# Earlier release of a batch's loads, its last keys in two pieces, and its TensorE steps spread over two output units, in a fused attention and SwiGLU kernel

## The chip, the cores and the metric

One core of one Trainium2 chip runs the whole program. The metric is the device time of one execution in microseconds. The granted clock, the share of TensorE's full speed that the profile records, has a mean of 0.99 to 1.00.

## The reference

An attention without a softmax over pairs feeds a gated feed-forward block.

```python
q_s = exp(q - max_d);  q_s /= sum_d            # softmax of each query over its 64 features
k_s = exp(k - max_s);  k_s /= sum_s            # softmax of the keys over the 576 positions
kv  = einsum('bhsd,bhse->bhde', k_s, v)        # 64 x 64 for each head
x   = einsum('bhsd,bhde->bhse', q_s, kv)       # laid out as 4608 tokens x 512
out = (silu(x @ w_gate) * (x @ w_val)) @ w_out # 512 -> 1536 -> 512
```

There are 8 batches of 8 heads, 576 positions and 64 features. Inputs are float32; the kernel computes in bfloat16 on TensorE (PE).

## The kernel before

Work is written in the order in which each engine takes it. Batch 0's 576 tokens go first, through twelve units (called m-units): each has a gate and a value product into two PSUM banks, which ScalarE (ACT, the silu `sg`) and VectorE (DVE, the product `hr`) then empty. After that comes the stretch that the change rewrites: the four output projections of batch 0's first 512 tokens, with batch 1's attention between them. Then follows the first regular chunk (448 tokens), into which batch 2's attention is worked.

```python
psp = ctx.enter_context(tc.tile_pool(name="psp", bufs=8, space=PSUM))   # 8 banks, used in turn
...
def load_kv(b):
    for G in range(NG):                       # NG = 2 groups of four heads
        load("k", k, b, G)
        load("v", v, b, G)
...
for c0, n in ((0, 128), (128, 128), (256, 128), (384, 128), (512, 256), (768, 384), (1152, 384)):
    w_slice(wg, moe_w_gate, c0, n)            # GpSimd queue, float32 -> bf16 on the way
    w_slice(wv, moe_w_val, c0, n)
w_dma = [wo_slice(m0, 3) for m0 in (0, 3, 6, 9)]
...
after = w_dma[-3]                             # batch 1's loads wait for the 2nd output-weight slice
for what, src in (("q", q), ("v", v), ("k", k)):
    for G in range(NG):
        load(what, src, 1, G, after=after)
        after = None
load("q", q, 2, 0); load("q", q, 2, 1); load_kv(2)

for m in range(MT):
    m_unit(0, S, m, by_group=(m == 0))        # batch 0: twelve units

exp_of("q", 1, 0); exp_of("q", 1, 1)          # ACT, after a switch of its function table
norm_sum(1, 0); i = norm_mul(1, 0)            # DVE; norm_mul writes qs
cast_v(1, 0)
c = cast_v(1, 1)                              # GpSimd (POOL), float32 -> bf16
tc.add_manual_dep(c.ins, i.ins.name, ...)     # second cast after the first product
norm_sum(1, 1)
o_out(0, o_mm(0), nc.scalar); o_out(1, o_mm(1), nc.scalar)
exp_of("k", 1, 0)
turn_pe(1, 0, 0); turn_pe(1, 0, 1)            # PE transposes of qs
...
kv_both(1); scale_both(1)                     # keys x values, then kn on DVE
...
exp_of("k", 2, 0); exp_of("k", 2, 1)          # before ACT switches its table to silu
...
for m in range(MT):                           # the first chunk (ci == 0)
    ...                                       # m == 5: kv_both(2); m == 6: exp_of("k", 3, 0), ("k", 3, 1)
    m_unit(c0, n, m, by_group=(ci == 0 and m == 0))
    if att and m == 9:
        x_and_next_kv(b)                      # the x step, with the next batch's keys x values
```

In the profiles `eq` and `ek` are the exponentials of queries and keys, `qs` the normalised queries, `qt` their transposes, `vb` the values in bfloat16, `kv` and `kn` the key-value product before and after its scaling, `xp` the x step and `xt` its result; `g_ps`, `u_ps` and `o_ps` are PSUM banks of the gate, value and output products.

The softmax here doesn't subtract the row's maximum and nothing guards it: scores larger than these inputs give would overflow.

Of the kernel before, what the change touches and what calls it, by code (L numbers as in the profile page):

```python
# [15 lines left out]
def kernel(  # L16
# [10 lines left out]
    nc = tc.nc  # L27
# [5 lines left out]
    MT = d_ff // 128  # L33
    T = S // 64
# [3 lines left out]
    BANKS = ((0, 5), (5, T))  # L38
# [8 lines left out]
    def bank(name):  # L47
        return psp.tile([128, 512], FP32, tag="ps", name=name)
# [16 lines left out]
    def head_ap(src, b, G, t0=0, t1=T):  # L65
        return bass.AP(
            tensor=src.tensor,
            offset=src[b, 4 * G].offset + 64 * t0,
            ap=[[T * 64, 128], [2 * HSTR, 2], [1, (t1 - t0) * 64]],
        )  # L70

    def load(what, src, b, G, pieces=((0, T),), after=None):
        t_ = ld.tile([128, 2, T * 64], FP32, tag=what, name=what)
        raw[what, b, G] = t_
        last = None
        for t0, t1 in pieces:
            last = nc.sync.dma_start(out=t_[:, :, 64 * t0:64 * t1], in_=head_ap(src, b, G, t0, t1))  # L77
            if after is not None:
                tc.add_manual_dep(last.ins, after.ins.name, SYNC, reason="order of loads")
                after = None  # L80
        return last
# [6 lines left out]
    def w_slice(dst, src, c0, n):  # L88
        ap = bass.AP(
            tensor=src.tensor,  # L90
            offset=src[0, c0].offset,
            ap=[[d_ff, 128], [128 * d_ff, KT], [1, n]],
        )
        return nc.gpsimd.dma_start(out=dst[:, :, c0:c0 + n], in_=ap)  # L94

    def wo_slice(m0, n):
        ap = bass.AP(
            tensor=moe_w_out.tensor,
            offset=moe_w_out[m0 * 128, 0].offset,
            ap=[[d_model, 128], [128 * d_model, n], [1, d_model]],  # L100
        )
        return nc.gpsimd.dma_start(out=wo[:, m0:m0 + n, :], in_=ap)

    def copy(eng, out, in_):
        if eng is nc.scalar:
            nc.scalar.copy(out=out, in_=in_)
        else:
            eng.tensor_copy(out=out, in_=in_)  # L108
# [3 lines left out]
    st = {}  # L112

    def exp_of(what, b, G, pieces=((0, T),)):
        s = st.setdefault((b, G), {})
        e = s["e" + what] = at.tile([128, T, 2, 64], BF16, tag="e" + what, name="e" + what)
        src = raw[what, b, G].rearrange("p h (t d) -> p t h d", d=64)
        for t0, t1 in pieces:
            nc.scalar.activation(out=e[:, t0:t1], in_=src[:, t0:t1], func=AF.Exp)  # L119
# [34 lines left out]
    def turn_pe(b, G, i):  # L154
        s = st[b, G]
        if i == 0:
            s["qt"] = at.tile([128, T, 128], BF16, tag="qt", name="qt")
        t0, t1 = BANKS[i]
        tp = s["tp", i] = psp.tile([128, 1024], BF16, tag="ps", name="tp")
        for t in range(t0, t1):  # L160
            j = t - t0
            nc.tensor.transpose(
                out=tp[:, j * 128:(j + 1) * 128], in_=s["qs"][:, t, :], identity=ident
            )

    def turn_out(b, G, i, eng):
        s = st[b, G]
        t0, t1 = BANKS[i]
        copy(
            eng,  # L170
            s["qt"][:, t0:t1, :],
            s["tp", i][:, 0:(t1 - t0) * 128].rearrange("p (t c) -> p t c", c=128),
        )
# [8 lines left out]
    def kv_mm(b, G, kv, c):  # L182
        ek = st[b, G]["ek"]
        for t in range(T):
            for g in range(2):
                for h in range(2):
                    nc.tensor.matmul(  # L187
                        out=kv[g][HALF[h], c:c + 65], lhsT=ek[HALF[g], t, h, :],
                        rhs=vbs[G][HALF[g], t, h, :],
                        start=(t == 0), stop=(t == T - 1),  # L190
                    )
# [23 lines left out]


    def kv_both(b):
        kv = st["kv", b] = [bank("kv") for _ in range(2)]
        for G in range(NG):
            kv_mm(b, G, kv, 256 * G)  # L220

    def scale_both(b):
        kn = st["kn", b] = at.tile([128, 2, NG, 64], BF16, tag="kn2", name="kn2")
# [67 lines left out]
    def store(j, o_sb, c0=0, c1=512, engs=(nc.sync, nc.sync)):  # L291
        for half in range(2):
            b, t = divmod(2 * j + half, T)
            dst = bass.AP(
                tensor=out.tensor,
                offset=out[b * S + t, c0].offset,
                ap=[[T * d_model, 64], [1, c1 - c0]],
            )
            engs[half].dma_start(out=dst, in_=o_sb[64 * half:64 * half + 64, c0:c1])

    def o_mm(j, o_ps=None, m0=0, m1=MT):
        if o_ps is None:
            o_ps = bank("o_ps")
        r0 = (j * 128) % RING
        for m in range(m0, m1):
            nc.tensor.matmul(  # L306
                out=o_ps, lhsT=hr[:, m, r0:r0 + 128], rhs=wo[:, m, :],
                start=(m == 0), stop=(m == MT - 1),
            )
        return o_ps  # L310

    def o_out(j, o_ps, eng=nc.vector):
        o_sb = osb.tile([128, 512], FP32, tag="o_sb", name="o_sb")
        copy(eng, o_sb, o_ps)
        store(j, o_sb)

    def o_unit(j):
        o_out(j, o_mm(j))
# [17 lines left out]
    with tc.manual_schedule():  # L336
# [23 lines left out]
        norm_mul(0, 0, BANKS)  # L360
        norm_sum(0, 1, BANKS)

        for c0, n in ((0, 128), (128, 128), (256, 128), (384, 128), (512, 256), (768, 384), (1152, 384)):
            w_slice(wg, moe_w_gate, c0, n)
            w_slice(wv, moe_w_val, c0, n)
        w_dma = [wo_slice(m0, 3) for m0 in (0, 3, 6, 9)]
# [67 lines left out]
        x_out(0, 1, 0, xp1[0])  # L434
        x_out(0, 1, 1, xp1[1])

        after = w_dma[-3]
        for what, src in (("q", q), ("v", v), ("k", k)):
            for G in range(NG):
                load(what, src, 1, G, after=after)  # L440
                after = None
        load("q", q, 2, 0)
        load("q", q, 2, 1)
# [13 lines left out]
        o_out(0, o_mm(0), nc.scalar)  # L457
        o_out(1, o_mm(1), nc.scalar)
        exp_of("k", 1, 0)
        turn_pe(1, 0, 0)  # L460
        turn_pe(1, 0, 1)
        turn_out(1, 0, 0, nc.scalar)
        exp_of("k", 1, 1)
        norm_mul(1, 1)
        p = o_mm(2)
        turn_out(1, 0, 1, nc.vector)
        turn_pe(1, 1, 0)
        turn_pe(1, 1, 1)
        turn_out(1, 1, 0, nc.scalar)
        turn_out(1, 1, 1, nc.vector)  # L470
        kv_both(1)
        scale_both(1)
        o_out(2, p, nc.scalar)
        exp_of("q", 2, 0)
        p = o_mm(3, m1=MT // 2)
        x_and_next_kv(1, with_kv=False)
        o_mm(3, p, m0=MT // 2)
        o_out(3, p)
        exp_of("q", 2, 1)
        norm_sum(2, 0)  # L480
        norm_mul(2, 0)
# [9 lines left out]
        for ci, (c0, n) in enumerate(chunks):  # L491
            b = ci + 2
            jo = 4 * ci
            att = b < B
            more = b + 1 < B
            final = ci == len(chunks) - 1
            for m in range(MT):
                if ci == 0:
                    if m == 3:
                        norm_mul(b, 1)  # L500
                        turn_dma(b, 1)
                    elif m == 5:
                        kv_both(b)
                        scale_both(b)
                    elif m == 6:
                        exp_of("k", b + 1, 0)
                        exp_of("k", b + 1, 1)
                        cast_v(b + 1, 0)
                        cast_v(b + 1, 1)
                elif m == 3:  # L510
                    if att:
                        exp_of("q", b, 0)
                        exp_of("q", b, 1)
                        norm_sum(b, 0)
                    o_unit(jo)
                    if att:
                        norm_mul(b, 0)
                        turn_dma(b, 0)
                    o_unit(jo + 1)
                    if att:  # L520
                        norm_sum(b, 1)
                elif m == 4 and att:
                    norm_mul(b, 1)
                    turn_dma(b, 1)
                elif m == 7:
                    if more:
                        exp_of("k", b + 1, 0)
                        exp_of("k", b + 1, 1)
                        cast_v(b + 1, 0)
                        cast_v(b + 1, 1)  # L530
                    o_unit(jo + 2)
                    if not final:
                        o_unit(jo + 3)
                if m == 8 and more:
                    for G in range(NG):
                        load("q", q, b + 1, G)
                    if b + 2 < B:
                        load_kv(b + 2)
                m_unit(c0, n, m, by_group=(ci == 0 and m == 0))
                if att and m == 9:  # L540
                    x_and_next_kv(b)
        o_unit(jo + 3)
        last = n_tok // 128 - 4
# [33 lines left out]
```

## Time and profile before

| what | before | view |
|---|---|---|
| time, median of the first 3 runs | 313.84 us | runs |
| PE busy | 97% of the span | page |
| stretch of output units | 37.81 to 52.47 us, 14.66 us | PE timeline |
| its first m-unit to the next chunk | 52.47 to 73.08 us, 20.61 us | PE timeline |
| batch 2's last keys land | 54.9 us | issue plus latency of that load |

The page of the kernel before: busy time of the engines in us with its share of the span and the number of instructions (PEld is TensorE's loading of weights), then the chain of waits by engine.

```profile
PE 301.5 (97%) x2158; PEld 150.6 (48%) x2182; DVE 160.5 (51%) x273; ACT 146.2 (47%) x214; POOL 33.1 (11%) x41
...
PE 80%; DMA 11%; ACT 2%; POOL 2%; issue 1%; SPq 1%; DVE 1%; DVEq 0%; ACTq 0%
```

PE bounds the kernel, so a change of order can win only what PE waits. The PE timeline of the kernel before, in the stretch: start, duration, line, operation, count, and in brackets the idle time before it and what ended it.

```profile
37.81 5.34 PE L306 MATMUL o_ps<-wo,hr 128*128 128x512 bf16 x23
43.67 0.68 PE L162 MATMUL tp<-ident,qs 128*128 128x128 bf16 x9 [0.51 <-DVE qs L147]
44.18 2.75 PE L306 MATMUL o_ps<-wo,hr 128*128 128x512 bf16 x12
46.97 0.68 PE L162 MATMUL tp<-ident,qs 128*128 128x128 bf16 x9
47.58 0.48 PE L187 MATMUL kv<-vb,ek 64*64 64x65 bf16 x36
48.73 0.48 PE L187 MATMUL kv<-vb,ek 64*64 64x65 bf16 x36 [0.67 <-ACT ek L119]
49.37 1.24 PE L306 MATMUL o_ps<-wo,hr 128*128 128x512 bf16 x5 [0.16 <-issue]
50.54 0.69 PE L242 MATMUL xp<-qt,kn 64*64 64x512 bf16 x16
51.16 1.47 PE L306 MATMUL o_ps<-wo,hr 128*128 128x512 bf16 x6
52.47 0.54 PE L281 MATMUL g_ps<-xt,wg 128*128 128x448 bf16 x2
```

The brackets add up to 1.34 us, about 1.4 with gaps too small for a bracket. The ACT timeline of the kernel before shows what comes next: the keys of batch 2 must be done before ACT loads its silu table.

```profile
54.92 1.16 ACT L119 ACTIVATE ek<-k 128x1152 bf16<-128x1152 f32 x1 [0.57 <-DMA k<-in_k_dram]
56.10 1.28 ACT L288 ACT_TABLE_LOAD   x1
57.40 1.42 ACT L288 ACTIVATE sg<-g_ps 128x448 bf16<-128x448 f32 x3
```

An m-unit takes PE 1.51 us, and eight banks hold four units: a PE that starts at 52.47 needs its first bank back at about 58.5, and gets it. The windows of the kernel before (per microsecond: busy times, last the bytes written in GB/s) show the DMA system while batch 1 loads:

```profile
35.00:36.00 1.00, 1.00 (x11) 0.79 (x9) 0.00 (x0) 0.68 (x2) 0.00 (x0) 1.00 1.19 223
36.00:37.00 1.00, 1.00 (x11) 0.80 (x9) 0.82 (x2) 0.08 (x1) 0.00 (x0) 1.00 1.08 321
37.00:38.00 1.00, 1.00 (x9) 0.75 (x8) 0.03 (x1) 0.98 (x3) 0.00 (x0) 1.00 1.07 395
```

Last, the timeline of the kernel before for DVE's query products and POOL's value casts:

```profile
42.88 2.82 POOL L122 CAST vb<-v 128x1152 bf16<-128x1152 f32 x2 [19.39 <-DMA v<-in_v_dram]
45.20 1.71 DVE L147 TENSOR_TENSOR qs<-eq,rr 128x1152 bf16<-128x1152 bf16 x1
```

### The profile page before, as it was taken

To read this page: it belongs to the slowest core of one execution; us is meant where nothing else is said; L and a number is where in the kernel's file an instruction comes from. 1 tells how busy PE (TensorE), PEld (TensorE's weight loads), DVE (VectorE), ACT (ScalarE), POOL (GpSimd) and SP (SyncE) were. 2 spreads that over 40 slices of the span, in tenths; PEclk is the share of its full clock that TensorE was granted. 3 is DMA by queue.
4 is the path that set the end of the run, shared out by engine and by line. 5 is a ranking of instruction groups with operands and counts; after the bars stand their busy time and mean duration, and the time that the engine had idled before them with its cause. 6 is when DMAs were issued, how large, how long until landed. Compare 5 with 4: busy or idle time off the path is not lost.

```text
span 312.1 us, 5426 instructions
## 1 busy us (share of the span) xinstructions
PE 301.5 (97%) x2158; PEld 150.6 (48%) x2182; DVE 160.5 (51%) x273; ACT 146.2 (47%) x214; POOL 33.1 (11%) x41
## 2 busy tenths in 40 slices
PE   6999998999999999999999999999999999999994
PEld 2687744554444444444444444544444444444443
DVE  3844476945763567355826492639353324333321
ACT  5743559693764465547464737455043113212200
POOL 2980031120200110002000200000000000000000
PEclk9999999999999999999999999999999999999998
DMA  7999999899256906491739252605310202021034
GB/s 272 191 191 204 272 395 392 292 243 391 70 99 148 375 17 130 102 382 42 143 68 357 97 119 62 185 1 106 72 34 0 69 21 46 3 67 25 9 73 100
DMA packets 42475, 45.78 MB, mean 147 GB/s; under 512 B 20561, under 2 KB 26193, under 8 KB 42449
## 3 DMA queue, kind: packets, MB, share of 16 engines
q1 hardware_dynamic: 32480, 39.99, 43.4%
q0 software_dynamic: 9808, 5.31, 12.4%
q8 instruction: 17, 0.28, 0.4%
q10 hardware_dynamic: 160, 0.13, 0.2%
q14 instruction: 10, 0.07, 0.1%
HBM read 37.75 MB, written 9.44 MB: 151 GB/s over the span
## 4 chain that ended last, share of the span: by engine, by line
PE 80%; DMA 11%; ACT 2%; POOL 2%; issue 1%; SPq 1%; DVE 1%; DVEq 0%; ACTq 0%
PE o_ps L306 26%; PE g_ps L281 25%; PE u_ps L281 25%; DMA k<-in_k_dram 5%; DMA wo<-in_moe_w_out_dram 4%; DMA wv<-in_moe_w_val_dram 2%; PE kv L187 1%; PE xp L242 1%; ACT ek L119 1%; PE o_ps L326 1%; SPq L77 1%; POOL wv L94 1%; POOL wg L94 1%; DVE hr L289 0%; POOL v L344 0%
## 5 line engine op out<-in xcount | busy, mean ns | idle before, releaser
L288 ACT ACTIVATE sg<-g_ps 128x512 bf16<-128x512 f32 (+2 forms) x120 | 64.6, 554 | 134.7 <-PE g_ps L281 133.2
L289 DVE TENSOR_TENSOR hr<-sg,u_ps 128x512 bf16<-128x512 bf16 (+2 forms) x120 | 74.2, 630 | 88.3 <-PE u_ps L281 81.1
L281 PE MATMUL g_ps<-xt,wg 128*128 128x512 bf16 (+2 forms) x473 | 110.9, 358 | 0.5
L281 PE MATMUL u_ps<-xt,wv 128*128 128x512 bf16 (+2 forms) x479 | 111.1, 358 | 0.1
L306 PE MATMUL o_ps<-wo,hr 128*128 128x512 bf16 x404 | 92.6, 379 | 0.9 <-issue 0.2
L281 PEld LDWEIGHTS <-wv 128*128 128x128 bf16 x480 | 47.0, 98 | 46.4
L281 PEld LDWEIGHTS <-wg 128*128 128x128 bf16 x480 | 46.4, 98 | 45.4 <-issue 0.2
L306 PEld LDWEIGHTS <-hr 128*128 128x128 bf16 x420 | 40.9, 98 | 48.7
L108 DVE COPY o_sb<-o_ps 128x512 f32<-128x512 f32 x32 | 21.8, 680 | 39.4 <-PE o_ps L306 35.7
L122 POOL CAST vb<-v 128x1152 bf16<-128x1152 f32 x14 | 16.6, 1193 | 137.0 <-DMA v<-in_v_dram 120.1
L133 DVE TENSOR_REDUCE rs<-eq 128x18 f32<-128x1152 bf16 (+2 forms) x18 | 21.7, 1214 | 13.1 <-ACT eq L119 13.0
L147 DVE TENSOR_TENSOR qs<-eq,rr 128x1152 bf16<-128x1152 bf16 (+2 forms) x18 | 22.1, 1235 | 0.1
L119 ACT ACTIVATE eq<-q 128x1152 bf16<-128x1152 f32 (+2 forms) x18 | 18.3, 1052 | 3.9 <-DMA q<-in_q_dram 3.9
L119 ACT ACTIVATE ek<-k 128x1152 bf16<-128x1152 f32 x16 | 18.1, 1159 | 2.9 <-DMA k<-in_k_dram 2.9
L288 ACT ACT_TABLE_LOAD x12 | 15.4, 1283 | 0.2
L119 ACT ACT_TABLE_LOAD x11 | 14.1, 1283 | 0.2
L371 PE MATMUL idle<-zero 128*128 128x512 bf16 x20 | 7.8, 555 | 2.7 <-DVE rs L133 1.5
L257 DVE CAST xt<-xp 128x512 bf16<-128x512 f32 x14 | 9.0, 681 | 0.9 <-PE xp L242 0.9
L256 ACT CAST xt<-xp 128x512 bf16<-128x512 f32 x14 | 7.9, 586 | 3.3 <-PE xp L242 3.3
L187 PE MATMUL kv<-vb,ek 64*64 64x65 bf16 x504 | 6.9, 194 | 0.7 <-ACT ek L119 0.7
L187 PEld LDWEIGHTS <-ek 64*64 64x64 bf16 x504 | 6.4, 107 | 2.1 <-ACT ek L119 0.8
L242 PE MATMUL xp<-qt,kn 64*64 64x512 bf16 (+1 forms) x112 | 6.7, 292 | 0.0
(43 smaller groups left out, 65.7 us busy)
## 6 DMA issues: line engine op xcount, KB each, us to landing
q<-in_q_dram SPq DMA_DIRECT2D x16, 576.0 KB, 5.3
k<-in_k_dram SPq DMA_DIRECT2D x16, 576.0 KB, 7.8
out_dram<-o_sb SPq DMA_DIRECT2D x70, 128.0 KB, 2.3
v<-in_v_dram SPq DMA_DIRECT2D x14, 576.0 KB, 8.8
wo<-in_moe_w_out_dram POOLq DMA_DIRECT2D x4, 384.0 KB, 14.1
wg<-in_moe_w_gate_dram POOLq DMA_DIRECT2D x2, 384.0 KB, 9.3
wv<-in_moe_w_val_dram POOLq DMA_DIRECT2D x2, 384.0 KB, 10.2
wg<-in_moe_w_gate_dram POOLq DMA_DIRECT2D x4, 128.0 KB, 5.4
```

What stands on the lines that cost most here:

```text
L108: eng.tensor_copy(out=out, in_=in_)
L119: nc.scalar.activation(out=e[:, t0:t1], in_=src[:, t0:t1], func=AF.Exp)
L122: return nc.gpsimd.tensor_copy(out=vbs[G][:, :, :, 0:64], in_=raw["v", b, G].rearrange("p h (t d) -> p t h d", d=64),)
L133: i = nc.vector.reduce_sum(out=rs[:, 2 * t0:2 * t1], in_=eq2[:, 2 * t0:2 * t1, :], axis=mybir.AxisListType.X)
L147: last = eng.tensor_mul(qs[:, t0:t1, :].rearrange("p t (h d) -> p (t h) d", d=64), eq2[:, 2 * t0:2 * t1, :], s["rr"][:, 2 * t0:2 * t1].to_ ...
L187: nc.tensor.matmul(out=kv[g][HALF[h], c:c + 65], lhsT=ek[HALF[g], t, h, :], rhs=vbs[G][HALF[g], t, h, :], start=(t == 0), stop=(t == T - 1),)
L242: nc.tensor.matmul(out=o[h][HALF[g], c:c + 64 * (t1 - t0)], lhsT=kn[HALF[h], g, G, :], rhs=qt[G][HALF[h], t0:t1, 64 * g:64 * g + 64], star ...
L257: nc.vector.tensor_copy(out=xt[:, 2 * G + 1, c0:c0 + 512], in_=main[G][1])
L281: nc.tensor.matmul(out=gu[a][i][:, 0:w_], lhsT=(wg, wv)[a][:, kk, ms], rhs=xt[:, kk, c:c + w_], start=(kk == 0), stop=(kk == KT - 1),)
L288: nc.scalar.activation(out=sg[:, 0:w_], in_=g_ps[:, 0:w_], func=AF.Silu)
L289: nc.vector.tensor_mul(hr[:, m, r:r + w_], sg[:, 0:w_], u_ps[:, 0:w_])
L306: nc.tensor.matmul(out=o_ps, lhsT=hr[:, m, r0:r0 + 128], rhs=wo[:, m, :], start=(m == 0), stop=(m == MT - 1),)
```

## The change

The intent: start batch 1's loads sooner, and cut PE's waits in the stretch by placing pieces of the third and fourth output units between the attention steps. Three edits concern loads, one concerns PE order, and one moves the x step of the first chunk.

```diff
-        for c0, n in ((0, 128), (128, 128), (256, 128), (384, 128), (512, 256), (768, 384), (1152, 384)):
+        for c0, n in ((0, 128), (128, 128), (256, 256), (512, 256), (768, 384), (1152, 384)):
...
-        after = w_dma[-3]
+        after = w_dma[0]
...
-                load(what, src, 1, G, after=after)
+                split = what == "k" and G == 1
+                load(what, src, 1, G, BANKS if split else ((0, T),), after=after)
...
         exp_of("k", 1, 0)
+        p2 = o_mm(2, m1=4)
         turn_pe(1, 0, 0)
         turn_pe(1, 0, 1)
         turn_out(1, 0, 0, nc.scalar)
-        exp_of("k", 1, 1)
+        exp_of("k", 1, 1, BANKS)
         norm_mul(1, 1)
-        p = o_mm(2)
+        o_mm(2, p2, m0=4)
...
+        st["kv", 1] = [bank("kv") for _ in range(2)]
+        p3 = o_mm(3, m1=4)
+        o_out(2, p2)
         kv_both(1)
         scale_both(1)
-        o_out(2, p, nc.scalar)
         exp_of("q", 2, 0)
-        p = o_mm(3, m1=MT // 2)
+        o_mm(3, p3, m0=4, m1=10)
         x_and_next_kv(1, with_kv=False)
-        o_mm(3, p, m0=MT // 2)
-        o_out(3, p)
+        o_mm(3, p3, m0=10)
+        o_out(3, p3)
...
-                if att and m == 9:
+                if att and m == (10 if ci == 0 else 9):
                     x_and_next_kv(b)
```

More of the change, by code (lines that the diff above doesn't have):

```diff
@@ L217, in kv_both @@
     def kv_both(b):
-        kv = st["kv", b] = [bank("kv") for _ in range(2)]
+        if ("kv", b) not in st:
+            st["kv", b] = [bank("kv") for _ in range(2)]
         for G in range(NG):
-            kv_mm(b, G, kv, 256 * G)
+            kv_mm(b, G, st["kv", b], 256 * G)
     def scale_both(b):
```

## The prediction

> **What bounds it now.** TensorE. The page gives PE 97% busy, the chain of waits is 80% PE. The windows and the PE timeline place what little idleness there is: after the warm-up (until 14.3 us) PE runs without a gap to 37.8 us, and again from 52.5 us. Between lies the stretch that the change rewrites: four out-projection units plus batch 1's attention, 37.81 to 52.47 us = 14.66 us. Its work is 48 matmuls of 216 ns (10.4), 18 transposes (1.1), key-value 2 x 0.5 and x 0.62: about 13.2 us. Idle: 0.51 (waits for the first `qs`, DVE), 0.67 (waits for the last `ek`, ACT), 0.16 and small ones: about 1.4 us. Another 0.2-0.3 us lies at 60 and 68.5-70 us, where PSUM banks wait for ACT/DVE. So about 1.7 us (0.5%) is all that can be won; the change touches nothing else of 314 us.
>
> **What the change moves.**
> 1. Four weight slices (128 columns) become two of 256. Slices of 128 land 0.72 us apart, later ones at 206 GB/s (1.25 us per 256): the weight stream ends 0.4 us earlier. The Trainium skill ("DMA: Bandwidth & Descriptors", Specifications) says that transfers below 512 B miss line rate; the trace agrees: about 175 GB/s at 11-18 us, 205 later. Price: the third gate unit (PE at 18.2 us) now needs 256 columns, landing at about 18.3, the value slice at about 19.5 (needed 19.3). Estimated stall 0.1-0.4 us, where there was none.
> 2. Loads are released by the first output-weight slice. It landed at 32.15, the second at 34.0; now about 31.8. Release moves 2.2 us. While both kinds of load ran (36-37 us) writes rose from 206 to 321 GB/s and the last weight slice still landed on pace (1.9 us), so an early release gains transfer time: estimated 0.6-1 us for `k`, with step 1 1.0-1.4 (first `k` 45.85 -> about 44.7). The skill (same page, queues) has queues share engines round-robin, so the last output slice (landed 37.8, needed 39.8) can slip to 39-41; a stall up to 0.8 us in unit 0 is possible.
> 3. PE order: four matmuls of unit 2 now cover the wait for `qs`; unit 2's other eight, the second transposes; four of unit 3 cover `ek`; six cover `kn`; two the `xt` copies. `ek` in two pieces costs one ACT instruction (about 0.1 us). One 0.6 us eviction goes from ACT to DVE.
> 4. The next batch's x step goes one unit later, removing perhaps 0.1-0.2 us of waiting for banks.
>
> **On the critical path.** The limit becomes DVE: table load to 39, `eq`, then two sums, reciprocals and products end at about 46.5 us; PE reaches the second transposes at about 46.4. The earlier `v` casts (POOL) may collide with the first product; before, the second product took 1.71 instead of 1.36 us beside a cast. I expect 0.2-0.5 us of gaps left in the stretch, m-units starting at 51.2-51.7 instead of 52.47, and nothing returned later, since `k` of batch 2 (landed 54.9, gating ACT's table switch) also comes about 1 us earlier.
>
> Sum: 1.4 idle + 0.25 later - 0.25 weight stall - 0.4 residual = 1.0 us. Predicted 312.8 us, range 312.2 to 313.5; faster by over 2% 0.01, within 2% 0.98, slower 0.01.
>
> **What would show it.** First `eq` load landing before 38 us; first `k` near 44.7; no PE wait for `ek`; m-units near 51.4; sg after the first table switch about 0.5-1 us earlier than 57.4; PE gap near 18.2/19.3 (step 1's price); possibly a gap near 40 us on the last output slice.
>
> **What would make it wrong.** Output slices delayed beyond 41 us: gain eaten (about 313.8). PE running into the banks held until ACT leaves its exponentials (57 us): gain returned. If neither price appears, 312.2.

## The result, and the profile after

The median was 313.37 us (313.23 to 314.21, 6 runs) against 313.93 (313.80 to 315.02, 6 runs) for before. The ratio is 0.9981, with a 95% interval of 0.9963 to 0.9998. Run again as one of the experiments (e9), the changed kernel gave 313.56 against 313.75, ratio 0.9996 (0.9983 to 1.0008). The ratios are not quite the ratios of the medians. By the medians the change is worth 0.56 us in the first measurement and 0.19 us in the second; the intervals alone allow a gain of up to 1.2 us in the first, and in the second anything from a gain of 0.5 us to a loss of 0.3 us.

The page of the changed kernel:

```profile
PE 301.7 (97%) x2182; PEld 149.7 (48%) x2182; DVE 161.3 (52%) x274; ACT 145.9 (47%) x214; POOL 31.2 (10%) x39
```

The PE timeline of the changed kernel, in the stretch, then in the fifth m-unit:

```profile
37.65 6.21 PE L307 MATMUL o_ps<-wo,hr 128*128 128x512 bf16 x28
43.69 0.67 PE L162 MATMUL tp<-ident,qs 128*128 128x128 bf16 x9
44.19 1.89 PE L307 MATMUL o_ps<-wo,hr 128*128 128x512 bf16 x8
46.72 0.68 PE L162 MATMUL tp<-ident,qs 128*128 128x128 bf16 x9 [0.64 <-DVE qs L147]
47.23 1.03 PE L307 MATMUL o_ps<-wo,hr 128*128 128x512 bf16 x4
48.19 0.90 PE L187 MATMUL kv<-vb,ek 64*64 64x65 bf16 x72
49.02 1.47 PE L307 MATMUL o_ps<-wo,hr 128*128 128x512 bf16 x6
50.42 0.69 PE L243 MATMUL xp<-qt,kn 64*64 64x512 bf16 x16
51.04 0.61 PE L307 MATMUL o_ps<-wo,hr 128*128 128x512 bf16 x2
51.51 0.54 PE L282 MATMUL g_ps<-xt,wg 128*128 128x448 bf16 x2
...
57.98 0.92 PE L282 MATMUL g_ps<-xt,wg 128*128 128x448 bf16 x4 [0.26 <-ACT sg L289]
```

One gap is left of three, 0.64 us before the second transposes. The stretch took 13.86 us (37.65 to 51.51), 0.80 less than before. But the fifth m-unit starts 6.47 us after the first; in before it was 6.05 (52.47 to 58.52 us). So 0.42 us is lost there, 0.26 of it marked. The ACT timeline of the changed kernel says why:

```profile
54.91 1.16 ACT L119 ACTIVATE ek<-k 128x1152 bf16<-128x1152 f32 x1 [0.68 <-DMA k<-in_k_dram]
56.09 1.28 ACT L289 ACT_TABLE_LOAD   x1
57.39 1.42 ACT L289 ACTIVATE sg<-g_ps 128x448 bf16<-128x448 f32 x3
```

The three starts agree with before to 0.01 us: PE came 0.96 us earlier, ACT did not. Two of the windows of the changed kernel:

```profile
35.00:36.00 1.00, 1.00 (x11) 0.80 (x9) 0.15 (x1) 0.51 (x2) 0.00 (x0) 1.00 1.11 298
...
37.00:38.00 1.00, 1.00 (x9) 0.69 (x8) 0.19 (x1) 0.98 (x3) 0.00 (x0) 1.00 1.07 368
```

More is written at 35 us and less at 37 us. The landings (issue plus the latency that the trace gives for that one load, in us) show what the earlier release bought:

| | before | changed |
|---|---|---|
| first and last output-weight slice | 32.1, 37.8 | 31.3, 39.2 |
| first load of batch 1 issued | 34.03 | 31.26 |
| batch 1's q | 39.3, 40.8 | 38.3, 40.1 |
| batch 1's v | 42.9, 44.4 | 42.7, 44.2 |
| batch 1's k | 45.9, 47.3 | 45.7, then 46.6 and 47.3 |
| batch 2's last k | 54.9 | 54.8 |

The loads were issued 2.8 us earlier, but the first keys landed only 0.2 us earlier and the last ones no earlier at all; all trace times before the stretch lie about 0.1 to 0.16 us earlier in this execution anyway. The first q won 1.0 us, and the last weight slice lost 1.4 us.

The timeline of the changed kernel for the casts and the second product:

```profile
44.31 1.15 POOL L122 CAST vb<-v 128x1152 bf16<-128x1152 f32 x1 [0.28 <-DVE rs L133]
44.62 2.04 DVE L147 TENSOR_TENSOR qs<-eq,rr 128x1152 bf16<-128x1152 bf16 x1
```

The product takes 2.04 us, against 1.36 for the same operation elsewhere.

### The profile page after: what moved, and what is told of

Same layout as the page of the kernel before. It is cut to its first block, busy times and chain, and to the rows that moved or that the text cites. A ratio compares the mean times of both kernels' runs of the same rounds, so it can differ in the third digit from the quotient of the medians. Undisturbed runs are those within 1.5% of the kernel's fastest.

```text
span 311.3 us, 5449 instructions
## 1 busy us (share of the span) xinstructions
PE 301.7 (97%) x2182; PEld 149.7 (48%) x2182; DVE 161.3 (52%) x274; ACT 145.9 (47%) x214; POOL 31.2 (10%) x39
## 3 DMA queue, kind: packets, MB, share of 16 engines
q0 software_dynamic: 8752, 5.31, 11.9%
## 4 chain that ended last, share of the span: by engine, by line
PE 80%; DMA 12%; POOL 4%; ACT 1%; SPq 1%; issue 0%; DVE 0%; ACTq 0%
PE o_ps L307 26%; PE g_ps L282 26%; PE u_ps L282 25%; DMA k<-in_k_dram 8%; DMA wo<-in_moe_w_out_dram 4%; POOL wg L94 1%; POOL wv L94 1%; PE kv L187 1%; PE xp L243 1%; PE o_ps L327 1%; ACT ek L119 1%; SPq L77 1%; POOL v L345 0%; ACT L289 0%; POOL v L342 0%
## 5 line engine op out<-in xcount | busy, mean ns | idle before, releaser
L307 PE MATMUL o_ps<-wo,hr 128*128 128x512 bf16 x420 | 93.9, 379 | 0.0
L307 PEld LDWEIGHTS <-hr 128*128 128x128 bf16 x420 | 40.8, 98 | 48.6
L108 DVE COPY o_sb<-o_ps 128x512 f32<-128x512 f32 x33 | 22.4, 680 | 39.2 <-PE o_ps L307 39.2
L119 ACT ACTIVATE ek<-k 128x1152 bf16<-128x1152 f32 (+2 forms) x17 | 18.3, 1102 | 3.4 <-DMA k<-in_k_dram 3.3
L289 ACT ACT_TABLE_LOAD x12 | 15.4, 1283 | 0.2
L119 ACT ACT_TABLE_LOAD x11 | 14.1, 1283 | 0.2
L372 PE MATMUL idle<-zero 128*128 128x512 bf16 x20 | 6.5, 480 | 2.7 <-DVE rs L133 1.4
```

Of the source, the lines that this page charges most:

```text
L108: eng.tensor_copy(out=out, in_=in_)
L119: nc.scalar.activation(out=e[:, t0:t1], in_=src[:, t0:t1], func=AF.Exp)
L289: nc.scalar.activation(out=sg[:, 0:w_], in_=g_ps[:, 0:w_], func=AF.Silu)
L307: nc.tensor.matmul(out=o_ps, lhsT=hr[:, m, r0:r0 + 128], rhs=wo[:, m, :], start=(m == 0), stop=(m == MT - 1),)
```

## The experiments

The experiments ran in three groups (e1 to e4, e5 to e8, e9 to e12), on three chips, each beside its own runs of before; times are compared within a group.

Single executions vary a great deal before the stretch: the first gate unit starts anywhere from 13.8 to 15.0 us in these profiles, and the order of the program there differs in no way that would explain it. So each profile is also read by the lengths of its stages, differences of starts in the PE timeline. From the next chunk on, the kernels compared agree within 0.02 us on when the last group of matmuls begins (before 231.66 us after that chunk's start, changed 231.65).

| profile | twelve units | stretch | first m-unit to next chunk | sum of the last two |
|---|---|---|---|---|
| before | 23.53 | 14.66 | 20.61 | 35.27 |
| changed | 23.53 | 13.86 | 20.82 | 34.68 |
| e1 loads only | 23.54 | 14.58 | 20.82 | 35.40 |
| e2 order and x | 23.89 | 13.71 | 21.06 | 34.77 |
| e3 order only | 23.53 | 14.18 | 21.67 | 35.85 |
| e4 x only | 23.53 | 14.37 | 20.40 | 34.77 |
| e5 cast later | 23.78 | 13.50 | 21.98 | 35.48 |
| e6 keys first | 23.89 | 13.62 | 20.68 | 34.30 |
| e7 cast and keys | 23.53 | 14.07 | 20.39 | 34.46 |
| e8 late gate | 23.53 | 13.81 | 20.76 | 34.57 |
| e9 changed again | 23.63 | 13.61 | 21.68 | 35.29 |
| e10 gates moved | 23.53 | 13.08 | 20.40 | 33.48 |
| e11 gates moved, old order | 23.53 | 15.00 | 20.40 | 35.40 |
| e12 gates moved, old loads | 23.53 | 13.57 | 20.40 | 33.97 |

Theory, formed from the two traces: the DMA stream is conserved, so the load edits win nothing (C); what PE wins in the stretch is held back where it runs into PSUM banks that ACT frees only after a table switch, and that switch hangs on the landing of the next keys (G). The rivals: the earlier loads are what the change wins by (L); each part adds its own gain (A).

### e1: the loads alone

```diff
+ the three load edits of the change; everything else as before
```

> Before plus the three load changes alone (two 256-column slices in place of four of 128, release by the first output-weight slice, last keys in two pieces); the PE order is the old one. Theory C (the DMA stream is conserved: it was saturated, so releasing it earlier only makes the weight slices and the loads share it): first q lands about 1 us earlier, all later loads within 0.2 us of before, last output-weight slice about 1.4 us later, time within 0.15 us of before. Rival L (the earlier loads are what the change wins by): first keys well before 45.5 us in the trace and time 0.4 us or more below before.

Measured: 314.25 us against 313.79, ratio 1.0015 (1.0003 to 1.0028). The keys landed as theory C said, the first at 45.9 us and batch 2's last at 55.0, within 0.2 us of before. The two others had the expected direction, not the size: the first q came at 38.8 us, 0.5 us earlier where 1 was expected, and the last output-weight slice at 39.9, 2.0 us later where 1.4 was expected. Rival L falls. The time missed: 0.15% slower, where equal was expected. The profile shows only 0.13 us of it in the stages (35.40 against 35.27, with 0.22 us of waiting for batch 2's transposed queries in the x step). Where the rest comes from in the other runs is not settled.

One part of it can be seen. In each profile with the keys in two pieces less was loaded between 44 and 46 us. The DMA view of that window for the kernel before (packets, MB, share):

```profile
q1 hardware_dynamic: 358, 0.79, 105.7%
```

and for the changed kernel:

```profile
q1 hardware_dynamic: 504, 0.75, 108.5%
```

It was 0.78 to 0.79 MB in all six profiles with whole keys and 0.74 to 0.75 in all eight with split ones, 0.04 MB or about 0.1 us of the stream. The Trainium skill ("DMA: Bandwidth & Descriptors", Why small descriptors are slow) gives each packet a fixed overhead of about 3 cycles beside one cycle for 32 bytes. An estimate from that, with rows of 1280 and 1024 bytes in place of 2304, is a rate some 4% lower for what is moved in such rows. Only one load of 0.59 MB is split here, and 0.04 MB is 7% of it: the direction agrees, the loss is larger than the estimate.

### e2, e3, e4: order and x step, order alone, x step alone

```diff
  e2: the changed kernel with the three load edits undone
  e3: as e2, and
- if att and m == (10 if ci == 0 else 9):
+ if att and m == 9:
  e4: before, and
- if att and m == 9:
+ if att and m == (10 if ci == 0 else 9):
```

> The changed kernel with all three load changes undone: only the new PE order and the x step one unit later remain. Theory C: as fast as the changed kernel, so 0.4 to 0.7 us below before; m-units start near 51.6 us; a wait of about 0.3 us at the fifth m-unit, because the first sg stays at 57.4. Rival L: at most 0.2 us below before.

> As e2, with the x step back after the tenth m-unit. Theory G (PE time won in the stretch is held back at the next place where PSUM banks wait for ACT after a table switch): PE reaches the x step about 0.5 us earlier than before but waits there, and the x step starts within 0.25 us of before's 68.5; time at most 0.3 us below before. Rival A (the parts add up: order about 0.5, x about 0.2): 0.45 us or more below before.

> Before with the x step one unit later and nothing else. Both theories: 0.1 to 0.25 us below before, the x step with its key-value products taking about 1.3 us of PE instead of 1.53, and no wait before it. If it gives nothing, the x step had cost nothing in before either, and its worth in the changed kernel is only that it lets the order's gain through.

Measured beside the same runs of before (313.79 us): e2 313.94, ratio 1.0004 (0.9989 to 1.0018); e3 314.17, ratio 1.0011 (0.9999 to 1.0024); e4 313.41, ratio 0.9986 (0.9973 to 0.9999).

e2 missed: 0.4 to 0.7 us was expected, nothing came. Its stretch is as short as in the changed kernel (13.71 us), and it did not wait at the fifth m-unit as expected, since batch 2's last keys landed at 54.4 us and the first `sg` came at 56.95 instead of 57.4; but the profiled execution waited 0.30 us for `sg` at the eleventh m-unit, and 0.36 us over the twelve units before the stretch, where a weight slice came late. The second is not the order's doing.

e3 bears theory G out in direction, and its time refutes rival A. The stretch shrank by 0.48 us, but the fifth m-unit came 6.33 us after the first (6.05 in before), so 0.28 us was lost there. The x step began at 68.00 instead of 68.53 us (I had expected it within 0.25 of 68.5), and the rest of the wait fell inside the step. The PE timeline of e3:

```profile
68.00 0.84 PE L243 MATMUL xp<-qt,kn 64*64 64x512 bf16 x4
68.66 0.69 PE L187 MATMUL kv<-vb,ek 64*64 64x65 bf16 x36
69.31 0.41 PE L243 MATMUL xp<-qt,kn 64*64 64x512 bf16 x4
```

The second group begins 1.31 us after the first, against 0.59 in before (68.53 and 69.12). The ACT timeline of e3 shows why:

```profile
64.93 1.16 ACT L119 ACTIVATE ek<-k 128x1152 bf16<-128x1152 f32 x1 [0.67 <-DMA k<-in_k_dram]
66.11 1.28 ACT L289 ACT_TABLE_LOAD   x1
67.40 1.85 ACT L289 ACTIVATE sg<-g_ps 128x448 bf16<-128x448 f32 x4
```

This is gate G a second time: the table switch waits for the last keys of batch 3, the first `sg` comes 0.18 us later than in before (67.22) though PE came 0.53 us earlier, and the `sg` of four units, which fill all eight banks, end only at 69.25 us; the second group starts 0.06 us later. Its transposed queries had landed at 68.9 us, so they did not hold it.

They can be a gate of their own. In e1 the second group waited for them, by the PE timeline of e1:

```profile
69.48 0.41 PE L242 MATMUL xp<-qt,kn 64*64 64x512 bf16 x4 [0.22 <-DMA qt<-qs]
```

They landed at 69.4 us in e1, at 69.0 in before, and between 68.1 and 70.3 in the others.

e4 came as expected: the x step with what follows it costs 0.21 us less, the whole gain of the medians is 0.38 us, and its runs spread by only 0.42 us. One line of the change, alone, did as well as the whole.

### e5, e6, e7: the second cast later, keys first, both

```diff
  e5: the changed kernel, and
         cast_v(1, 0)
-        c = cast_v(1, 1)
-        tc.add_manual_dep(c.ins, i.ins.name, SYNC, ...)
 ...
-        norm_mul(1, 1)
+        i = norm_mul(1, 1)
+        c = cast_v(1, 1)
+        tc.add_manual_dep(c.ins, i.ins.name, SYNC, ...)
  e6: the changed kernel, and
     def load_kv(b):
         for G in range(NG):
             load("k", k, b, G)
+        for G in range(NG):
             load("v", v, b, G)
  e7: both
```

> The changed kernel, with the second v cast (POOL) of batch 1 held until the second query product (DVE) is done, so that the two do not overlap. Theory: the 2.04 us of that product were 1.36 of work and the rest a wait for the port that both use; the product now takes 1.35 to 1.40 us, the PE gap before the second transposes (0.64 us) shrinks to under 0.1, m-units start about 0.5 to 0.6 us earlier (near 50.95). Theory G (PE is then held back by the first sg at 57.4, which hangs on the landing of batch 2's last keys): the wait at the fifth m-unit grows from 0.42 to about 0.9-1.0 us and the time stays within 0.15 us of the changed kernel. Rival A: 0.5 us below the changed kernel.

> The changed kernel, with both key loads of a batch issued ahead of its two value loads (from batch 2 on). Theory G: batch 2's last keys land about 1.4 us earlier (53.4 instead of 54.8), the first sg about 0.7 us earlier (56.7 instead of 57.4), the wait at the fifth m-unit (0.42 us) goes, batch 3's last keys also about 1.5 us earlier; the time is 0.3 to 0.5 us below the changed kernel. Rival (the first sg is not what holds the fifth m-unit, or the values then come late): no gain, or a new wait of the key-value products of batch 2 for the v cast.

> Both edits of e5 and e6. Theory G: with the gate moved, the time won in the stretch counts: about 0.9 to 1.1 us below the changed kernel (about 312.3), more than the sum of e5 and e6 taken alone. Rival A: the sum of the two single gains and no more.

Measured beside the same runs of before (313.71 us): e5 313.69, ratio 1.0003 (0.9981 to 1.0025); e6 313.38, ratio 0.9980 (0.9959 to 1.0001); e7 313.44, ratio 0.9984 (0.9964 to 1.0004).

e5: the product took 1.36 us and no PE gap before the second transposes was left, so the cause of the 2.04 us is shown. The stretch fell to 13.50 us. The time did not fall: the profiled execution then waited 0.29 us at the fifth m-unit and 0.83 at the eleventh, both for `sg`. The expectation named only the first of these two places; and the wait there did not grow to 0.9 us, because m-units started at 51.69 us and not at 50.95: that execution was 0.29 us late from the first gate unit on, lost 0.25 more over the twelve units, and waited 0.29 us in the stretch for the last output-weight slice, which landed at 40.4 us. Rival A falls here too, as far as the runs of before show it; the changed kernel did not run beside e5.

e6: batch 2's last keys landed at 53.6 us, the first `sg` came at 56.90, and no wait at the fifth m-unit was left; of the time won there 0.28 us went in the x step, where the transposed queries landed at 70.2 us. The time was 0.2% below before, as was the changed kernel's in its first measurement; whether it beats the changed kernel is not settled by these runs.

e7 missed its 312.3 us. The waits for `sg` were gone (20.39 us to the next chunk, the shortest of all), but in that execution the first value landed earlier, and its cast met the first product instead. The timeline of e7:

```profile
41.90 1.14 POOL L123 CAST vb<-v 128x1152 bf16<-128x1152 f32 x1 [19.08 <-DMA v<-in_v_dram]
41.97 2.28 DVE L148 TENSOR_TENSOR qs<-eq,rr 128x1152 bf16<-128x1152 bf16 x1
```

The collision had only moved. An order between two engines that rests on when a DMA lands is no order.

### e8, e9: late release, and the changed kernel again

```diff
  e8: the changed kernel, and
-        after = w_dma[0]
+        after = w_dma[-3]
  e9: the changed kernel, no edit
```

> The changed kernel with the release of batch 1's loads put back to the second output-weight slice; nothing else undone. Theory C: the first q lands about 0.5-0.7 us later (about 39), so the first exponential starts at the landing instead of after the table load, about 0.2-0.4 us later; keys within 0.2 us; that shifts the chain of sums and products by the same and so the second transposes; m-units start 0.1 to 0.4 us later, but the fifth m-unit's wait shrinks by as much: time within 0.15 us of the changed kernel. Rival L: 0.4 us slower.

> The changed kernel as it is, run again beside the three below on one chip. Expected 0.2 to 0.6 us below before, as the first time.

Measured: e8 313.69 us against 313.71, ratio 0.9998 (0.9980 to 1.0016). Its first q landed at 39.4 us instead of 38.3, its first keys at 45.6, the stretch was 13.81 us (changed 13.86). The gate's position wins nothing that can be seen. It can cost something: in three of the seven profiles with the early release the last output-weight slice came too late for the tenth matmul of the first output unit, which started 0.29 us late in e5 and e6 (slice at 40.4 us) and 0.11 us late in e1 (39.9). e9: 313.56 us against 313.75, ratio 0.9996 (0.9983 to 1.0008), so 0.19 us by the medians, just short of what was expected, and next to nothing by the means.

The profile of e9 fell on its slowest execution (314.48 us), which is the best witness for theory G: the same program, with the same stretch as e2 and e6, only with batch 2's last keys landing at 55.8 us instead of 54.8. The ACT timeline of e9:

```profile
55.84 1.16 ACT L119 ACTIVATE ek<-k 128x1152 bf16<-128x1152 f32 x1 [1.45 <-DMA k<-in_k_dram]
57.02 1.28 ACT L289 ACT_TABLE_LOAD   x1
58.32 0.54 ACT L289 ACTIVATE sg<-g_ps 128x448 bf16<-128x448 f32 x1
```

and its PE timeline:

```profile
58.91 0.92 PE L282 MATMUL g_ps<-xt,wg 128*128 128x448 bf16 x4 [1.02 <-ACT sg L289]
```

A landing 1.0 us later makes the first `sg` 0.93 us later, and the sum of the two stages 0.61 us longer than in the other profile of this kernel. Why that load took 8.9 us from its issue, where it took 7.9, the trace does not tell.

### e10, e11, e12: the gates moved

```diff
  e10: the changed kernel, and keys first as in e6, and
-        cast_v(1, 0)
-        c = cast_v(1, 1)
+        c = cast_v(1, 0)
         tc.add_manual_dep(c.ins, i.ins.name, SYNC, ...)
 ...
-        norm_mul(1, 1)
+        i = norm_mul(1, 1)
+        c = cast_v(1, 1)
+        tc.add_manual_dep(c.ins, i.ins.name, SYNC, ...)
  e11: these edits on before with the x step one unit later (old order, old loads)
  e12: e10 with the three load edits of the change undone
```

> The changed kernel with batch 2's and later key loads ahead of the values (as e6) and with each v cast of batch 1 held until the query product that it could collide with is done (as e5, but for both casts, since in e7 the collision had only moved to the first product: 2.28 us). Theory G: both products take about 1.36 us, the stretch of output units about 13.5 us (before 14.66, changed 13.86), from the first m-unit to the next chunk about 20.3 us (before 20.61, changed 20.82); time 0.6 to 1.0 us below the changed kernel, near 312.5. Rival (what the stretch wins is always given back, gates or not; or the spread of DMA landings hides it): within 0.3 us of the changed kernel.

> Before, with the x step one unit later and the same two edits as e10, but the old PE order and the old loads of the change. Theory G: the new PE order is worth something only where the gates let it through, so e10 is 0.6 to 1.0 us below this one, and this one is 0.3 to 0.6 us below before. Rival (order is worth nothing): equal to e10 within 0.3 us.

> e10 with the three load changes undone (four slices of 128, release by the second output-weight slice, last keys in one piece). Theory C: within 0.25 us of e10. Rival L: 0.4 us or more slower. If e1's loss (0.15% slower than before) was the loads' own, this one is 0.2 to 0.5 us faster than e10.

Measured beside e9 and the same runs of before (313.75 us): e10 312.72, ratio 0.9970 (0.9957 to 0.9983); e11 312.90, ratio 0.9984 (0.9968 to 1.0000); e12 313.12, ratio 0.9976 (0.9964 to 0.9988).

e10 came as expected and has the lowest median: 0.3% below before, and by the means of their runs (312.87 and 313.61) 0.73 us below the changed kernel beside it; the two intervals against before just meet. The timeline of e10 for casts and products:

```profile
43.95 1.14 POOL L123 CAST vb<-v 128x1152 bf16<-128x1152 f32 x1 [21.11 <-DVE qs L148]
45.48 1.36 DVE L148 TENSOR_TENSOR qs<-eq,rr 128x1152 bf16<-128x1152 bf16 x1
46.90 1.15 POOL L123 CAST vb<-v 128x1152 bf16<-128x1152 f32 x1 [1.80 <-DVE qs L148]
```

and its ACT timeline, to be held against the same three steps shown of before, changed and e9:

```profile
53.13 2.23 ACT L120 ACTIVATE ek<-k 128x1152 bf16<-128x1152 f32 x2
55.37 1.28 ACT L290 ACT_TABLE_LOAD   x1
56.67 2.03 ACT L290 ACTIVATE sg<-g_ps 128x448 bf16<-128x448 f32 x4
```

The two key exponentials run back to back, with no wait for a landing; the first `sg` comes 0.72 us earlier than in the changed kernel, and PE waits at none of the three gates. The stretch is 13.08 us, a little below the 13.2 us that the prediction called its bare work, and the sum of the stages is 1.79 us below before. In the profiled executions 1.1 us of it is left, since that of e10 began its first gate unit at 14.97 us, 0.69 us later than before's. By the means the time fell by 0.9 us; why not by more, the profiles do not tell.

e12 equals e10 within the intervals (0.12 us slower by the means, where at most 0.25 was expected, but 0.40 by the medians, which is where rival L began), so with the gates moved the load edits are still not seen to matter, and a small gain from them is not excluded; its profile had the lower total (312.39 us) only because its first gate unit began at 13.79 us. e11 lies 0.38 us above e10 by the means of the runs (313.25 and 312.87), less than the 0.6 to 1.0 expected, and the intervals overlap: that the new PE order pays once the gates are moved is likely from the stages of e10 and e12 (stretch 13.08 and 13.57 us against 14.37 to 15.00 with the old order), but the times do not settle it.

## Why the prediction was right or wrong

The range held (312.2 to 313.5, measured 313.37 at first and 313.56 the second time, the latter just outside), and so did "within 2%". The size did not: 1.0 us was predicted, and the medians show 0.56 and 0.19. That the range held is in part luck: its upper end lay only 0.3 us below before, so it left room for one of its terms to fail.

**What bounds it, and how much can be won: right.** PE idled about 1.4 us in the stretch. e10 recovered all of it (14.66 to 13.08 us).

**The stretch: the sum right, its share of the gain not.** Predicted were 1.4 us of idle less 0.4 left over, so 1.0; measured were 0.80 (changed) and 1.05 (e9). The residue in the changed kernel was where the prediction put it, before the second transposes, and larger: 0.64 us. Its cause was a value cast beside a query product, as feared, though the second product and not the first. The Trainium skill ("SBUF — State Buffer", Who interferes with whom) says that a DVE instruction with two SBUF inputs contends with a GpSimd instruction that reads SBUF, for a pair of ports that is locked as a whole, and that the order of issue decides which of the two blocks. The trace agrees: 2.04 us beside a cast, 1.36 with the cast held back (e5, e10), and 2.28 when both started together (e7). In before, changed and e7 alike the product ends 1.20 to 1.21 us after the cast does, so only about 0.15 of its 1.36 us was done beside the cast.

**Step 2, the earlier release: the term that failed.** "an early release gains transfer time: estimated 0.6-1 us for `k`, with step 1 1.0-1.4 (first `k` 45.85 -> about 44.7)". It landed at 45.7. The estimate read the rise from 206 to 321 GB/s while weights and loads overlapped as free capacity. It was a mix: the page counts 5.31 MB for the queue of the weights and of batch 0's values, their size in bfloat16, while twice as many float32 bytes are read, so a rise in written bytes is to be expected when plain loads take their place. The Trainium skill ("DMA: Bandwidth & Descriptors", Queues, rings and completion order) has each engine go round between the queues for which it has work, packet by packet. The trace agrees: the first q landed 1.0 us earlier, the last weight slice 1.4 us later (39.2 us, just ahead of its use at about 39.6), everything behind them about where it had been. e8 and e1 show the same.

**"Nothing returned later": failed with it.** The prediction made batch 2's keys come 1 us earlier, and so ACT's table switch. They landed at 54.8 us as before, the first `sg` stayed at 57.39, and PE gave back 0.42 us at the fifth unit. This was listed among what would make the prediction wrong ("PE running into the banks held until ACT leaves its exponentials (57 us)"), but weighed too lightly: the term "0.25 later" was to be a gain, and the stage measured 0.21 us longer in the changed kernel and 1.07 longer in e9. The skill's page "PSUM — Partial Sum Buffer" (Specifications (TRN2)) gives 8 banks per partition; the program uses all eight in turn, two for each unit, and the waits at the fifth unit and at the eleventh (in e3 at the x step in its place), each after a table switch, fit that.

**Step 4, the x step one unit later: right, and undersized.** 0.1 to 0.2 us was predicted; e4 shows 0.21 us in the stage and 0.14% in time, as much as the whole change. Its worth is what the prediction said, a wait for banks: in before the unit behind the step starts at 70.06 us, 0.38 us after the step's last matmuls began and just after DVE's last product of the tenth unit ended at 70.00; in the changed kernel it starts 0.18 us after them.

**Step 1, the price of wider slices: not seen in the changed kernel's first profile.** There was no stall at 18.2 or 19.3 us there. But two of the eight profiles with wider slices have a stall where the prediction named it, at the first wide value slice: e6 idles 0.16 us at 19.55 us (its twelve units took 0.36 us longer), e9 lost 0.1 us at 19.44. None of the six with the old slices has one there. e2's stall of 0.18 us at 16.57 is at a slice of 128 columns that both layouts share. So the price seems to exist and does not come every time; the few profiles do not settle its size.

Open: why e1 is 0.15% slower than before; how much the new order is worth by time once the gates are moved; and what makes a load, or the first 14 us, vary by a microsecond from one execution to the next. In e1's profile 0.11 us went with the late output-weight slice.

## What to carry to other kernels

Before an engine is made faster, find the next place where it waits for a buffer, and follow that wait to its source: here PE ran at most four units ahead of an ACT table switch that hung on a DMA landing, and the time won before it was returned there. In the saturated DMA stream of this kernel an earlier issue bought nothing, while the order of what is issued moved the gate (e6, e10), so load first what opens a gate (keys), then what has slack (values). Where two engines share a port, order them by a dependency between the two instructions, not by the landing of a load.

## What the Trainium skill lacked or had wrong

- "DMA: Bandwidth & Descriptors": it has no figure for a queue that casts sharing engines with one that does not. Here the casting weight loads alone wrote 195 to 214 GB/s of bfloat16 from 20 us on, plain loads 366 to 413 GB/s; released into the weights 2.8 us earlier, the loads won 1.0 us for the first, 0.2 us for the fifth and nothing for the sixth, and the last weight slice lost 1.4 us.
- The same page (Specifications) names 512 bytes as the least size for line rate. Rows of 1280 and 1024 bytes in place of 2304 still cost 0.04 MB (0.75 against 0.79 MB in 2 us), 7% of the one load that has such rows; the page's own section on small descriptors points that way, with about 4%.
- "ScalarE: Activation LUTs": Terms puts a table load at about 2.7 us; What ACT_TABLE_LOAD costs splits that into about 1283 ns for the load and about 1380 ns for a drain. The load is right (every profile here shows 1283 ns on average), the drain does not show: from the end of the last `ek` to the first `sg` only 1.32 us pass in before, changed and e9.
- No page tells how much the landing of one and the same load varies: batch 2's last keys landed 7.9 and 8.9 us after their issue in two executions of the changed kernel, and the first gate unit began between 13.8 and 15.0 us.
